# Short fp32 products of an attention and mixture-of-experts kernel issued as two halves of 64 stationary columns

## The chip, the cores and the metric

The kernel runs on one core of one Trainium2 chip, in one launch. The metric is the device time of that launch in microseconds (us); the median of three runs of the kernel before is 623.5 us (621.27 to 625.68).

## The reference

```python
def phi(x):                                   # x: (2, 8, 576, 64), scaled
    proj = np.einsum('bhsd,md->bhsm', x, omega)
    h = proj - np.sum(x * x, axis=-1, keepdims=True) / 2.0
    return np.exp(h - np.max(h, axis=-1, keepdims=True)) / np.sqrt(m)
kv = np.einsum('bhsm,bhsd->bhmd', k_p, v);  z = np.sum(k_p, axis=2)
num = np.einsum('bhsm,bhmd->bhsd', q_p, kv)
den = np.einsum('bhsm,bhm->bhs', q_p, z)[..., None] + 1e-06
x = (num / den)                               # laid out as 1152 tokens x 512
...
mask = e_idx == e                             # first expert layer: 8 experts, top 1
out[mask] = gate_w[mask, None] * eom[mask, e, None] * (np.maximum(x[mask] @ w1[e], 0.0) @ w2[e])
...
out += p[:, e:e + 1] * (np.maximum(x @ w1[e], 0.0) @ w2[e])   # second layer: 4 experts, all tokens
```

Everything is float32, with m = 128 features, 1152 tokens of 512 numbers and a hidden width of 1024.

## The kernel before

Most products are made from a high and a low part of each operand, as three fp32r products (`mm3`, lines 594 to 598; stage b, lines 295 to 297). A few are left as plain fp32 products, and these are what the change touches. A plain fp32 product shows in the trace as two passes, each with a weight load and a matmul.

The attention runs first. Its work goes in banks of 2 heads x 2 row sets for q and k, by batch b and half of the heads hh. `stage_a` transposes raw q or k (line 273) into the PSUM tile pt. `stage_b` multiplies with omega into pj (lines 295 to 297); VectorE takes the maximum and ScalarE the exponential (line 312). `kv_part` (line 326) sums k'v and z for four heads in the bank kv: the stationary operand is e, rows x 128 features, the moving one is v with a column of ones, 65 columns; the last 64 rows of a sequence (vr) go the same way with 64 rows. `kv_evac` copies the sum to kvs. `stage_cq` transposes the features of q (line 357), and `stage_d` (line 374) multiplies them with kvs into pnd, 65 columns again, divides, writes x to the DRAM tile xs and transposes it (line 385) into xh and xl. For the last 64 rows stage_d uses 64 stationary columns.

Then come the experts of the first layer, in chunks of 288 tokens: `l1` (tile ph), `l2_block` (tile py). One pair of a chunk and an expert with at most 64 tokens is gathered: line 805 picks the token rows with a one-hot matrix og into px (three token tiles x four column blocks), line 824 makes the first layer phx from raw fp32 weights xw1, line 832 the second, yx, and `scatter` (line 842) puts it back. Line 832 sends even f to output partitions 0 to 63 and odd f to 64 to 127:

```python
p0 = SLOTS * (f % 2)
mm = nc.tensor.matmul(yx[p0:p0 + SLOTS], hx[:, f], xw2[f // 4][:, f % 4, :], start=f < 2, stop=f >= FB - 2)
```

The buffers st of xw1 are reused for the second layer's weights xw2, whose DMAs (line 123) therefore wait for the products of line 824. A loop over the remaining pairs follows under a branch on nx (line 858), then the second expert layer (tiles pp and po).

The order of the instructions on each engine is made when the program is built, by a scheduler with its own costs, within the dependences; on the chip each engine takes them in that order.

Of the kernel before, what the change touches and what calls it, by code (L numbers as in the profile page):

```python
# [24 lines left out]
KB, FB = DM // 128, FF // 128  # L25
# [9 lines left out]
MXS = 8  # L35
SCALE = 1.0 / (D ** 0.25)
SLOT_J = (0, 2, 1, 3)


@with_exitstack  # L40
def moe_stack(ctx, tc, q, k, v, omega, w_gate, w_ogate, mw1, mw2, dprobs, dw1, dw2, out):
    nc = tc.nc
    TT, STT, TS = nc.vector.tensor_tensor, nc.vector.scalar_tensor_tensor, nc.vector.tensor_scalar

    def f32(ap):
        return ap.bitcast(F32)
# [97 lines left out]
    G = H // 2  # L144
# [135 lines left out]
    kvps = {}  # L280
# [41 lines left out]
    kvs = {}  # L322

    def kv_part(key, e, v65, first, last, r0, r1):
        for i in range(G):
            nc.tensor.matmul(kvps[key][:, i, :], e[i][r0:r1], v65[i],
                             start=first and i == 0, stop=last and i == G - 1)

    def kv_rest(b, hh):
        r = slice(64 * b, 64 * b + 64)  # L330
        vr = raw["v", 2]
        kv_part((b, hh), heads("k", 2, hh, 0), [vr[r, G * hh + i, :] for i in range(G)], False, True, r.start, r.stop)

    def stage_ck(u):
        kind, b, hh, j = u
        if b == 2:
            return kv_rest(0, hh)
        if j == 0:
            kvps[b, hh] = kbank[:, 0:G * (D + 1)].rearrange("p (g d) -> p g d", g=G)
        v65 = raw["v", b, hh]  # L340
        kv_part((b, hh), heads(*u), [v65[:, i, j, :] for i in range(G)], j == 0, False, 0, 128)
        if b == 1 and j == 3:
            kv_rest(1, hh)
# [21 lines left out]
    def stage_d(b, hh, u):  # L365

        t = st_e["T", u]
        rest = u[1] == 2
        m = 64 if rest else 128
        c0 = 64 * b if rest else 0  # L370
        bank = ps_n.tile([128, 512], F32, tag="nd", name="pnd")
        ps = bank[:, 0:G * (D + 1)].rearrange("p (g d) -> p g d", g=G)
        for i in range(G):
            nc.tensor.matmul(ps[:m, i, :], t[:, i, c0:c0 + m], kvs[b, hh][:, i, :], start=True, stop=True)

        rd = ap.tile([128, G], F32, tag="rd", name="rd", bufs=4)
        TS(rd[:m], ps[:m, :, D], M * 1e-6, None, op0=ALU.add)
        nc.vector.reciprocal(rd[:m], rd[:m])
        xn = ap.tile([128, G, D], F32, tag="xn", name="xn", bufs=4)
        TT(xn[:m], ps[:m, :, 0:D], rd[:m].unsqueeze(2).to_broadcast([m, G, D]), op=ALU.mult)  # L380
        dst = xs[8, 64 * b:64 * b + 64] if rest else xs[4 * b + SLOT_J[u[3]]]
        nc.sync.dma_start(dst[:, 256 * hh:256 * hh + 256], xn[:m].rearrange("p g d -> p (g d)"))
        px = bank[:, 0:256].rearrange("p (g n) -> p g n", g=2)
        for g in range(2):
            nc.tensor.transpose(px[:, g, :m], xn[:m, 2 * g:2 * g + 2, :].rearrange("p a d -> p (a d)"), ident[:m, :m])
        kbs = slice(2 * hh, 2 * hh + 2)
        if rest:
            cols = slice(S * b, S * b + S)
            dh, dl = (z[:, kbs, cols].rearrange("p k (c n) -> p k c n", c=2)[:, :, :, 256:NC] for z in (xh, xl))
            src = px[:, :, 0:64].rearrange("p k (c n) -> p k c n", c=2)  # L390
        else:
            s = SLOT_J[u[3]]
            col = S * b + NC * (s // 2) + 128 * (s % 2)
            dh, dl = (z[:, kbs, col:col + 128] for z in (xh, xl))
            src = px
        nc.scalar.copy(dh, src)
        x_done[b, hh, u[1:]] = TT(dl, src, f32(dh), op=ALU.subtract)
# [144 lines left out]
    def do_d(u):  # L542
        kind, b, hh, j = u
        if kind == "k":
            return
        if b < 2:
            cur["d"] = (b, hh)
        stage_d(*cur["d"], u)
        if b == 1 and j == 3:
            stage_d(1, hh, ("q", 2, hh, 0))  # L550
        if hh == 1 and (b == 2 or (b == 1 and j == 3)):
            gate(cur["d"][0])

    for st in range(n + LAGD + 2):
        if st < n:
            kind, b, hh, jp, hp = banks[st]
            if b < 2 and jp == 0 and hp == 0:
                squares(kind, b, hh, nc.vector if (kind, b, hh) == ("k", 0, 0) else nc.gpsimd)
                if kind == "k" and (b, hh) != (0, 0):
                    i = 2 * b + hh + 1  # L560
# [33 lines left out]
    def mm3(ps, st_hl, mv_hl, start, stop):  # L594
        (sh_, sl_), (mh, ml) = st_hl, mv_hl
        nc.tensor.matmul(ps, sh_, mh, start=start, stop=False)  # L596
        nc.tensor.matmul(ps, sh_, ml, start=False, stop=False)  # L597
        nc.tensor.matmul(ps, sl_, mh, start=False, stop=stop)  # L598
# [166 lines left out]
    xw1 = X.raw1()  # L765
    xt = [xg_.tile([128, DM], F32, tag="xt", name="xt", bufs=3) for _ in range(3)]
# [25 lines left out]
    og = xg_.tile([128, 3, SLOTS], F32, name="og")  # L792
# [9 lines left out]
    px = ps_n.tile([128, KB, SLOTS], F32, tag="nd", name="px")  # L802
    for kb in range(KB):
        for t in range(3):
            nc.tensor.matmul(px[:, kb], xt[t][:, 128 * kb:128 * kb + 128], og[:, t], start=t == 0, stop=t == 2)
    xg = xg_.tile([128, KB, SLOTS], F32, name="xg")
    nc.scalar.copy(xg, px)
    psx = ps_t.tile([128, 3, 128], F32, tag="pt", name="psx")
# [5 lines left out]
    e = nc.values_load(le_t[0:1, 0:1], engines=[SP], min_val=0, max_val=NE - 1)  # L814
# [4 lines left out]
    for q in range(2):  # L819
        pool, tag = RINGS[q]  # L820
        ps = pool.tile([128, 4, SLOTS], F32, tag=tag, name="phx")
        for i in range(4):
            for kb in range(KB):
                nc.tensor.matmul(ps[:, i], xw1[q][:, kb, 128 * i:128 * i + 128], xg[:, kb], start=kb == 0, stop=kb == KB - 1)
        nc.scalar.activation(hx[:, 4 * q:4 * q + 4], ps, AF.Relu)
    xw2 = X.raw2()

# [30 lines left out]
    with tc.If(nx > 0, preferred_fallthrough_block=True, label="more"):  # L858
        with tc.For_i(0, nx, 1) as it:
# [10 lines left out]
            t = lp.tile([128, 4, 2, NE], F32, tag="xt", name="xt")  # L870
# [12 lines left out]
    e = nc.values_load(ei[1][0:1, 0:1], engines=[SP], min_val=0, max_val=NE - 1)  # L883
# [148 lines left out]
    def layer2(e, j, g, h, w2):  # L1032
        for t in range(GROUPS[g][1] // 64):
# [3 lines left out]
            for i in range(2):  # L1037
                mm3(po, (h[i][0][:, ts_], h[i][1][:, ts_]), w2[i], i == 0, i == 1)
            b, jj = T // 4, SLOT_J[T % 4]
            pc = pb[:, 4 * b + jj if T < 8 else 8, e:e + 1]  # L1040
# [14 lines left out]
    for p in range(0, 4 * NE2, 2):  # L1055
        ej = [divmod(p + i, 4) for i in range(2)]
        ws = {}
        for i, g in ((0, 0), (1, 0), (0, 1), (1, 1)) if p == 0 else ((0, 0), (0, 1), (1, 0), (1, 1)):
            e, j = ej[i]
# [39 lines left out]
```

## Time and profile before

| | |
|---|---|
| median of 3 runs | 623.5 us (621.27 to 625.68) |
| the profiled execution | 623.27 us, of which the span from the first to the last instruction is 621.2 us |
| mean granted TensorE clock | 0.994 of 2.4 GHz |
| PE busy, PEld busy | 604.8 us (97%), 553.0 us (89%) |
| DVE, ACT, POOL busy | 407.8, 257.4, 259.8 us |

PE is TensorE's matmuls, PEld its weight loads. A matmul's busy time includes its way through the array, so successive matmuls overlap and the distance from start to start tells what one costs. In a name such as `kv<-v,e` the tile written stands first. `128*64 128x65` means 128 rows and 64 columns of stationary operand, and 65 moving columns on 128 partitions. Attention lies from the start to about 116 us, the first chunk of the first expert layer to about 150, the gathered pair from there to 184, the rest after that.

### The profile page before, as it was taken

The page shows a single profiled execution, that of the slowest core. Times are in us where ns is not written, and L with a number is a line of the kernel's source. Part 1 is how long each engine was busy: PE and PEld are TensorE (multiplying, and loading weights), DVE is VectorE, ACT ScalarE, POOL GpSimd, SP SyncE. Part 2 cuts the span into 40 slices and gives each one's busy share as a digit, 9 for nine tenths or more (in the row PEclk, how much of TensorE's full clock was granted, in tenths as well). Part 3 has the DMA queues.
Part 4 walks back from the last instruction along what each step waited for, and adds up shares of the span by engine and source line. Part 5 has one row for each costly group of instructions (what it writes and reads, how often), then busy time and mean ns, then how long its engine had stood idle before and what let it go on. Part 6 is the DMA issues. An engine that isn't in the chain of part 4 may idle for free.

```text
span 621.2 us, 10506 instructions
## 1 busy us (share of the span) xinstructions
PE 604.8 (97%) x3910; PEld 553.0 (89%) x3911; DVE 407.8 (66%) x937; ACT 257.4 (41%) x628; POOL 259.8 (42%) x302
## 2 busy tenths in 40 slices
PE   7989999999999998999999999999999999999996
PEld 6878899899969998999998998998998998998995
DVE  7686675886325588966676676676666666666564
ACT  4566676603214144544443443442442442442230
POOL 4995014400000004285753753753754754754220
PEclk9999999999999999999999999999999999999999
DMA  8731145007607020102202202102202202200004
GB/s 198 166 103 47 31 154 174 23 1 255 203 6 270 1 69 31 40 0 69 69 0 69 69 2 68 69 2 68 69 1 69 68 2 69 68 1 2 1 1 152
DMA packets 41238, 42.77 MB, mean 69 GB/s; under 512 B 14816, under 2 KB 29408, under 8 KB 41184
## 3 DMA queue, kind: packets, MB, share of 16 engines
q1 hardware_dynamic: 40896, 42.00, 21.5%
q8 instruction: 32, 0.52, 0.4%
q14 instruction: 22, 0.18, 0.1%
q10 hardware_dynamic: 288, 0.07, 0.0%
HBM read 37.34 MB, written 4.72 MB: 68 GB/s over the span
## 4 chain that ended last, share of the span: by engine, by line
PE 68%; DVE 1%; issue 0%; ACT 0%; ACTq 0%
PE po L597 11%; PE po L596 11%; PE po L598 11%; PE pp L596 9%; PE pp L598 9%; PE pp L597 9%; PE ph L596 1%; PE py L596 1%; PE py L598 1%; PE ph L598 1%; PE ph L597 1%; PE py L597 1%; DVE xcl L92 0%; DVE x2T L664 0%; DVE xl L92 0%; PE pg L629 0%
## 5 line engine op out<-in xcount | busy, mean ns | idle before, releaser
L92 POOL TENSOR_TENSOR wlo<-st,whi 128x512 fp32r<-128x512 f32 x100 | 120.6, 1229 | 228.6 <-ACT whi L91 223.8
L1044 DVE SCALAR_TENSOR_TENSOR oacc<-po,pb,oacc 128x512 f32<-128x512 f32 x135 | 99.9, 747 | 55.9 <-PE po L598 55.9
L91 ACT CAST whi<-st 128x512 fp32r<-128x512 f32 x120 | 67.9, 592 | 115.5 <-PE po L598 49.2
L597 PE MATMUL po<-wlo,hh 128*128 128x512 f32 x288 | 112.4, 390 | 0.0
L596 PE MATMUL po<-whi,hh 128*128 128x512 f32 x288 | 112.4, 390 | 0.0
L598 PE MATMUL po<-whi,hl 128*128 128x512 f32 x288 | 112.0, 389 | 0.0
L592 POOL TENSOR_TENSOR hl<-c,hh 128x320 fp32r<-128x320 f32 (+1 forms) x64 | 52.7, 824 | 87.0 <-ACT hh L591 74.0
L596 PE MATMUL pp<-xh,whi 128*128 128x320 f32 (+1 forms) x256 | 76.1, 297 | 0.0
L598 PE MATMUL pp<-xh,wlo 128*128 128x320 f32 (+1 forms) x256 | 76.1, 297 | 0.0
L597 PE MATMUL pp<-xl,whi 128*128 128x320 f32 (+1 forms) x256 | 76.1, 297 | 0.0
L598 PEld LDWEIGHTS po<-whi,hl 128*128 128x128 f32 x288 | 54.1, 188 | 11.3
L597 PEld LDWEIGHTS po<-wlo,hh 128*128 128x128 f32 x288 | 54.2, 188 | 10.1
L596 PEld LDWEIGHTS po<-whi,hh 128*128 128x128 f32 x288 | 54.2, 188 | 10.0
L991 DVE TENSOR_TENSOR c<-u,pp 128x320 f32<-128x320 f32 (+1 forms) x96 | 43.3, 453 | 22.1 <-PE pp L598 21.7
L596 PEld LDWEIGHTS pp<-xh,whi 128*128 128x128 f32 x256 | 48.8, 191 | 1.6 <-DVE u L1003 0.4
L597 PEld LDWEIGHTS pp<-xl,whi 128*128 128x128 f32 x256 | 48.8, 191 | 1.2
L590 ACT ACTIVATE c<-c 128x320 f32<-128x320 f32 (+1 forms) x64 | 28.5, 445 | 51.3 <-DVE c L991 50.5
L598 PEld LDWEIGHTS pp<-xh,wlo 128*128 128x128 f32 x256 | 48.8, 191 | 0.0
L312 ACT ACTIVATE e<-pj,nb 128x128 f32<-128x128 f32 x144 | 41.3, 378 | 15.7 <-DVE nb L305 14.8
L587 DVE SCALAR_TENSOR_TENSOR hl<-c,hh 128x320 fp32r<-128x320 f32 (+1 forms) x64 | 44.7, 733 | 0.2
L596 PE MATMUL ph<-xh,whi 128*128 128x288 f32 x128 | 38.2, 299 | 1.2 <-ACT dg L627 1.2
L596 PE MATMUL pp<-xch,whi 128*128 128x320 f32 (+1 forms) x128 | 38.1, 298 | 1.2 <-DVE c L991 1.2
(262 smaller groups left out, 1365.6 us busy)
## 6 DMA issues: line engine op xcount, KB each, us to landing
st<-in_moe_w_dram SPq DMA_DIRECT2D x32, 512.0 KB, 4.4
st<-in_moe_w_dram SPq DMA_DIRECT2D x10, 1024.0 KB, 5.6
v<-in_v_dram SPq DMA_DIRECT2D x16, 128.0 KB, 3.4
q<-in_q_dram SPq DMA_DIRECT2D x4, 512.0 KB, 4.7
xs<-xn SPq DMA_DIRECT2D x16, 128.0 KB, 1.7
own<-in_moe_w_dram SPq DMA_DIRECT2D x2, 1024.0 KB, 5.6
out_dram<-oacc SPq DMA_DIRECT2D x8, 256.0 KB, 2.1
k<-in_k_dram SPq DMA_DIRECT2D x3, 512.0 KB, 4.6
```

The lines of the kernel that those rows point to most:

```text
L91: nc.scalar.copy(hi, src)
L92: eng.tensor_tensor(lo, src, f32(hi), op=ALU.subtract)
L312: nc.scalar.activation(e[:, i // 2, i % 2], ps[:, i // 2, i % 2], AF.Exp, bias=nb[:, i // 2, i % 2:i % 2 + 1])
L587: STT(hl, src, 0.0, f32(hh), op0=ALU.max, op1=ALU.subtract)
L590: nc.scalar.activation(c, c, AF.Relu)
L592: nc.gpsimd.tensor_tensor(hl, c, f32(hh), op=ALU.subtract)
L596: nc.tensor.matmul(ps, sh_, mh, start=start, stop=False)
L597: nc.tensor.matmul(ps, sh_, ml, start=False, stop=False)
L598: nc.tensor.matmul(ps, sl_, mh, start=False, stop=stop)
L991: TT(c, u, p, op=op)
L1044: STT(oacc[:, T], po, pc, oacc[:, T], op0=ALU.mult, op1=ALU.add)
```

## The change

Four products with 128 stationary columns are each made as two with 64, the first for output partitions 0 to 63, the second for 64 to 127; the moving operand is the same for both. The products of line 374 for the last 64 rows had 64 columns already and stay.

```diff
+HALVES = (slice(0, 64), slice(64, 128))
...
     def kv_part(key, e, v65, first, last, r0, r1):
         for i in range(G):
-            nc.tensor.matmul(kvps[key][:, i, :], e[i][r0:r1], v65[i],
-                             start=first and i == 0, stop=last and i == G - 1)
+            for z in HALVES:
+                nc.tensor.matmul(kvps[key][z, i, :], e[i][r0:r1, z], v65[i],
+                                 start=first and i == 0, stop=last and i == G - 1)
...
         for i in range(G):
-            nc.tensor.matmul(ps[:m, i, :], t[:, i, c0:c0 + m], kvs[b, hh][:, i, :], start=True, stop=True)
+            for z in HALVES[:m // 64]:
+                nc.tensor.matmul(ps[z, i, :], t[:, i, c0 + z.start:c0 + z.stop], kvs[b, hh][:, i, :], start=True, stop=True)
...
         for t in range(3):
-            nc.tensor.matmul(px[:, kb], xt[t][:, 128 * kb:128 * kb + 128], og[:, t], start=t == 0, stop=t == 2)
+            for z in HALVES:
+                nc.tensor.matmul(px[z, kb], xt[t][:, 128 * kb + z.start:128 * kb + z.stop], og[:, t], start=t == 0, stop=t == 2)
...
             for kb in range(KB):
-                nc.tensor.matmul(ps[:, i], xw1[q][:, kb, 128 * i:128 * i + 128], xg[:, kb], start=kb == 0, stop=kb == KB - 1)
+                for z in HALVES:
+                    nc.tensor.matmul(ps[z, i], xw1[q][:, kb, 128 * i + z.start:128 * i + z.stop], xg[:, kb],
+                                     start=kb == 0, stop=kb == KB - 1)
```

On PE, the first k'v products (tile kv, from the features e of two banks) stand between the products with omega (tiles pj), before:

```order
L296 MATMUL pj_333<-oml_174,qTh_300 128x256
L326 MATMUL kv_181<-v0_120,e_201 128x65 x2
L326 MATMUL kv_181<-v0_120,e_226 128x65 x2
...
L297 MATMUL pj_333<-omh_173,qTl_301 128x256
L296 MATMUL pj_358<-oml_174,qTh_300 128x256
```

and after:

```order
L297 MATMUL pj_341<-oml_174,qTh_300 128x256
L328 MATMUL kv_181<-v0_120,e_201 64x65 x4
L328 MATMUL kv_181<-v0_120,e_226 64x65 x4
...
L298 MATMUL pj_341<-omh_173,qTl_301 128x256
L297 MATMUL pj_366<-oml_174,qTh_300 128x256
```

Eight products become sixteen in the same place, with the two halves of a product next to each other.

On PE, the first products of stage d (tiles pnd) lie among the transposes of q's features (tile pt, from e), before:

```order
L357 MATMUL pt_550<-ident_82,e_381 128x128 x2
L374 MATMUL pnd_564<-kvs_401,qpT_482 128x65 x4
L374 MATMUL pnd_579<-kvs_401,qpT_489 128x65 x2
L357 MATMUL pt_550<-ident_82,e_419 128x128
L374 MATMUL pnd_579<-kvs_401,qpT_489 128x65 x2
L295 MATMUL pj_535<-omh_173,qTh_453 128x256
```

and after:

```order
L359 MATMUL pt_570<-ident_82,e_397 128x128 x2
L377 MATMUL pnd_584<-kvs_421,qpT_502 64x65 x8
L377 MATMUL pnd_603<-kvs_421,qpT_509 64x65 x2
L359 MATMUL pt_570<-ident_82,e_439 128x128
L377 MATMUL pnd_603<-kvs_421,qpT_509 64x65 x5
L359 MATMUL pt_570<-ident_82,e_439 128x128
L377 MATMUL pnd_603<-kvs_421,qpT_509 64x65
```

Two stretches have become three (of 10, 5 and 1 halves), and one product's halves are parted.

On PE, the gathered pair's products px and phx stand among the second-layer products py, before:

```order
L805 MATMUL px<-og,xt 128x64
L596 MATMUL py<-hh,whi 128x288
L597 MATMUL py<-hl,whi 128x288
L805 MATMUL px<-og,xt 128x64
...
L805 MATMUL px<-og,xt 128x64 x10
L810 MATMUL psx<-ident,ogf 128x128
L598 MATMUL py<-hh,wlo 128x288
L596 MATMUL py<-hh,whi 128x288
L597 MATMUL py<-hl,whi 128x288
L824 MATMUL phx<-xg,st 128x64 x32
```

and after:

```order
L809 MATMUL px<-og,xt 64x64 x2
L599 MATMUL py<-hh,whi 128x288
L809 MATMUL px<-og,xt 64x64 x2
...
L809 MATMUL px<-og,xt 64x64 x20
L814 MATMUL psx<-ident,ogf 128x128
L601 MATMUL py<-hh,wlo 128x288
L599 MATMUL py<-hh,whi 128x288
L600 MATMUL py<-hl,whi 128x288
L829 MATMUL phx<-xg,st 64x64 x64
```

The places are nearly the same; px keeps three stretches and phx one.

## Rows read from the trace of the kernel before

**Rows 1.** The page: span, busy engines, and the chain by line.

```profile
span 621.2 us, 10506 instructions
...
PE 604.8 (97%) x3910; PEld 553.0 (89%) x3911; DVE 407.8 (66%) x937; ACT 257.4 (41%) x628; POOL 259.8 (42%) x302
...
PE po L597 11%; PE po L596 11%; PE po L598 11%; PE pp L596 9%; PE pp L598 9%; PE pp L597 9%; PE ph L596 1%; PE py L596 1%; PE py L598 1%; PE ph L598 1%; PE ph L597 1%; PE py L597 1%; DVE xcl L92 0%; DVE x2T L664 0%; DVE xl L92 0%; PE pg L629 0%
```

**Rows 2.** Busy us by stretch: length, PE, PEld, DVE, ACT, POOL (instructions), clock, DMA.

```profile
15.50:116.50 101.00, 96.49 (x771) 87.02 (x770) 70.24 (x242) 63.36 (x203) 48.63 (x67) 0.99 0.37 107
...
150.00:184.00 34.00, 33.86 (x240) 28.96 (x238) 12.20 (x39) 8.67 (x20) 0.00 (x0) 1.00 0.33 106
```

**Rows 3.** Waits of PE from 15.5 to 116.5 us: total, times, longest.

```profile
PE pj L295 <- ACT e L312: 1.9, 5, 0.6
PE pt L357 <- ACT e L312: 1.2, 3, 0.5
```

**Rows 4.** PE by shape, 15 to 116.5 us, then 150 to 185: busy us, mean ns.

```profile
L374 PE MATMUL pnd<-kvs,qpT 128*128 128x65 f32 x128 | 16.0, 271 | 0.0
L326 PE MATMUL kv<-v,e 128*128 128x65 f32 x128 | 15.6, 274 | 0.0
...
L326 PE MATMUL kv<-vr,e 64*128 64x65 f32 x32 | 4.4, 278 | 0.0
...
L824 PE MATMUL phx<-xg,st 128*128 128x64 f32 x64 | 7.4, 276 | 0.0
...
L805 PE MATMUL px<-og,xt 128*128 128x64 f32 x24 | 3.1, 271 | 0.0
```

**Rows 5.** Timeline of PE, 157.5 to 167 us: start, us, engine, line, tile, count.

```profile
158.74 7.36 PE L824 MATMUL phx<-xg,st 128*128 128x64 f32 x64
```

**Rows 6.** Timeline of PE around a stretch of k'v, 17.7 to 20.05 us.

```profile
17.84 0.28 PE L296 MATMUL pj<-oml,qTh 128*128 128x256 f32 x1
17.96 1.89 PE L326 MATMUL kv<-v,e 128*128 128x65 f32 x16
19.66 0.36 PE L297 MATMUL pj<-omh,qTl 128*128 128x256 f32 x1
```

**Rows 7.** Timeline of PE around stage d's last 64 rows, 44.05 to 45.3 us.

```profile
44.21 0.27 PE L273 MATMUL pt<-ident,qr 128*128 128x128 f32 x1
44.41 0.68 PE L374 MATMUL pnd<-kvs,qpT 128*64 128x65 f32 x8
45.02 0.33 PE L273 MATMUL pt<-ident,qr 128*128 128x128 f32 x1
45.19 0.38 PE L273 MATMUL pt<-ident,k 128*128 128x128 f32 x2
```

**Rows 8.** Timeline of PE around the first yx, 170.2 to 173.0 us.

```profile
170.34 0.30 PE L597 MATMUL py<-hl,whi 128*128 128x288 f32 x1
170.48 0.29 PE L598 MATMUL py<-hh,wlo 128*128 128x288 f32 x1
170.70 1.94 PE L832 MATMUL yx<-st,hx 128*64 128x512 f32 x8
172.57 0.40 PE L596 MATMUL py<-hh,whi 128*128 128x288 f32 x1
```

**Rows 9.** Timeline of PE, only what had started by 170.72 us.

```profile
170.70 0.65 PE L832 MATMUL yx<-st,hx 128*64 128x512 f32 x2
```

**Rows 10.** Timeline of PE, the products of scatter, 177.7 to 180.0 us.

```profile
177.92 2.10 PE L842 MATMUL pa<-back,ys 128*128 128x384 f32 x6
```

**Rows 11.** Timeline of SP's DMA issues, 155 to 185 us.

```profile
162.56 3.94 SPq L123 DMA_DIRECT2D st<-in_moe_w_dram  x2
```

**Rows 12.** DMA issues by tensor and size, the last number us from issue to landing.

```profile
st<-in_moe_w_dram SPq DMA_DIRECT2D x10, 1024.0 KB, 5.6
```

**Rows 13.** Timeline of PE, the second yx, 173.8 to 176.5 us.

```profile
174.23 1.94 PE L832 MATMUL yx<-st,hx 128*64 128x512 f32 x8
```

**Rows 14.** Timeline of PE after the branch, 183 to 186 us.

```profile
185.06 0.37 PE L596 MATMUL ph<-xh,whi 128*128 128x288 f32 x1 [1.21 <-ACT dg L627]
```

## The prediction

> **What bounds the kernel now.** I read the page first: its chain runs through PE's lines to the end, and PE is busy 97% of 621.2 us [rows 1]. A busy PE may still wait inside its matmuls, so I then read the stretches in which the changed products lie. From 15.5 to 116.5 us, the attention, PE is busy 96.5 of 101.0 us while DVE has 70.2 and ACT 63.4; from 150 to 184 us, the gathered pair, it is 33.9 of 34.0 [rows 2]. The waits of PE in the attention are five groups of 4.2 us together, the two largest 1.9 and 1.2, both for ScalarE's exponential [rows 3]. So PE sets the pace in both stretches, with other engines close behind in the first one. The reader is to see that a matmul less on PE counts here, but not all of it in the attention. The branch at 184 us is a fixed point: PE resumes at 185.06 us after it [rows 14], and all that follows is the same program, so what is gained or lost ahead of it is what the kernel gains or loses.
>
> **What a changed product costs now.** The shapes count the passes: 128 of pnd, 128 of kv with 128 rows, 32 of kv with 64 rows, 64 of phx, 24 of px, 376 in all [rows 4]. Their mean of 271 to 278 ns is no price, as they overlap. The distance is: 64 passes of phx in a row take 7.36 us, less the last one's 0.28, over 63, so 0.112 us each [rows 5]. The kv passes agree: sixteen from 17.96 until the next product really starts at 19.74 (19.66, plus 0.08 by which its 0.36 exceeds the usual 0.28) are 0.111 each, and neither end costs extra [rows 6]. That is 376 x 0.112 = 42.1 us of PE.
>
> What sets 0.112 is the weight load, not the 64 or 65 columns that stream: fp32 streams 384 columns in (2.10 - 0.49) / 5 = 0.322 us, 0.84 ns each, so 65 columns take 0.055 [rows 10]. With 64 stationary columns the load is shorter: stage d's last rows make 8 passes of 65 columns between 44.41 and 45.02; without 0.05 for the first load and 0.09 of the stretch's end (both below), 0.47 / 8 = 0.059 each [rows 7].
>
> **What two halves cost.** The trace has them: yx alternates the output halves. Two of its matmuls have started by 170.72, both from 170.70 [rows 9], and eight passes end after 1.94 us [rows 8]. One after the other, 512 columns at 0.84 ns would take 8 x 0.43 = 3.4 us; taking the last one's own 0.6 off, three more pairs take 1.34, 0.45 a pair. So two halves go through the array at once, with loads in parallel as well. But yx issues four instructions in 0.45 us, the new products would have to issue four in 0.06, and no row shows that pace. The bounds for a pair are therefore 0.055 us (the stream alone, both at once) and 2 x 0.059 = 0.118 (nothing overlaps, as in rows 7 where only one half exists). I take 0.060, near the row of one half, because the pairs of yx start at the same hundredth. A pair replaces a pass of 0.112: it saves 0.052, at the bounds from +0.057 to -0.006.
>
> **What each stretch adds.** Going between 128 and 64 stationary columns is not free. Before yx, the last py is streamed by 170.48 + 0.14 (the distance to its neighbour) = 170.62, and yx starts at 170.70: 0.08, then 0.05 for its first load (0.65 against 0.60). After it, the last pass begins at 172.05 and streams 0.43, and py comes at 172.57: 0.09, and 0.11 more for its load (0.40 against 0.29). Together 0.33 us [rows 8, 9]. Between transposes, which are 0.11 apart, it is 0.09 (44.32 to 44.41) + 0.05 + 0.09 + 0.06 (0.33 against 0.27) = 0.29 [rows 7]. Kv in its old shape paid nothing [rows 6]. In the new order, the changed products make 30 stretches in the attention (13 of kv, 17 of pnd, among them five of one half) and 4 in the gathered pair. Two of the kv stretches are the 64-row ones alone, which differ in shape from their neighbours before as well, and about three more border on a 16- or 64-row product that already changes the shape. So 25 new changes at 0.31 us are 7.8 us. Sixteen stretches or parts have an odd number, a half without partner: 16 x 0.058 = 0.9.
>
> **The sum on PE.** Attention: 288 x 0.052 = 15.0, less 7.8 and 0.9, is 6.3 us. Gathered pair: 88 x 0.052 = 4.6, less 4 x 0.33 = 1.3, is 3.3 us; almost all of it is the single long phx, px with stretches of 2, 2 and 20 halves comes out at zero.
>
> What is late next: in the attention, ACT's exponentials and DVE, which already hold PE 4.2 us and would be at 63 and 70 of 95 us instead of 101; DMAs of q, k and v land while PE works on the bank before. I count two thirds, 4.2 us; if the waits swallow all of it this is zero, with no wait it is 6.3. The order on the other engines changes in a few neighbours only, which I cost at nothing; at worst it adds a wait of the size of those in rows 3, 0.6 us. In the gathered pair no compute engine is near; but xw2's DMAs wait for phx. They are issued at 162.56 and 166.50 at the latest (3.94 for two) [rows 11] and a megabyte lands 5.6 us after its issue [rows 12], 172.1 against the second yx at 174.23 [rows 13], 2.1 us of slack. The second issue comes as much earlier as phx ends earlier, the first only half as much, so the two overlap more; both megabytes in sequence need about 10 us from the first issue, which leaves next to nothing. I take off 0.3, so 3.0 us. Behind yx nothing but PE's own queue waits.
>
> Sum: 4.2 + 3.0 = 7.2 us, less 0.4 for new waits of PE on fresh kvs and features when a stretch shrinks: 6.8. The profiled execution took 623.27 us (621.2 in the span and 2.1 around it), close to the median of 623.5, so the forecast is 623.3 - 6.8 = 616.5 us.
>
> **Rivals.** First, the halves don't overlap because PE can't issue faster. In rows 7 a load and a matmul come every 0.059 us, the fastest steady pace in the trace; if that is the pace of issue and not of the load, a pair costs 0.118. Then the attention gains 288 x -0.006 = -1.7, the gathered pair -0.5, and the changes of shape cost 7.8 and 1.3 more: -11.3 us on PE, of which about nine tenths reach the end, 633.5 us. It decides from a pair of 0.085 us on, where the sum on PE is zero (376 x 0.027 = 10.1 saved, 7.8 + 0.9 + 1.3 spent). For it: no row with four short instructions so close. Against: yx's pairs start at one time, though they had 0.4 us to be prepared. The Trainium skill has a rule of this kind ("TensorE: Matmul & The Clock Gate", section "Wait — 56ns, not 53.3ns?"): with hardware decode off, the sequencer spends about 62 ns on each matmul, which binds when the array needs less. By it a pair would take an estimated 124 ns and the kernel some 636 us; rows 7's pace lies just below 62, so the trace bears it out little, and its chance is inside the 0.2 of this rival.
>
> Second, the attention is held by ACT and DVE as soon as PE gets shorter, so only the gathered pair's 3.0 us come: 620.3 us. For it: the waits for exponentials exist already [rows 3]. Against: 4.2 us of waits in 101, and DVE has 30 us spare [rows 2]. A pair of some 0.08 us, between the bounds, lands there too: 376 x 0.032 = 12.0 saved, 10 spent, about 621.5.
>
> That the change doesn't do what it says is hardly a case: the order of the new program has the 64-column products.
>
> **Chances.** Forecast 0.55 (own range 612 to 620), gain lost in the attention or a pair in between 0.25, no overlap 0.2. A measurement of this kernel can tell about 1% (6.2 us) from no change. Of the forecast's 0.55, 0.42 lie below 617.3 and 0.13 in the band; of the second case 0.02 below, 0.20 in the band, 0.03 above; the third is above. That gives 0.44, 0.33, 0.23. The range reaches from 611.5 (all of the 9.6 us arrives and pairs take 0.055, 376 x 0.005 = 1.9 more) to 632, into the no-overlap case.
>
> **What would show it.** Right: phx as 128 passes in a stretch of about 4 us instead of 7.4, two matmuls of it starting within 0.01 us; gaps of 0.09 us at both ends of each kv and pnd stretch; the branch 6 to 7 us earlier. Wrong: phx in 7 to 8 us, that is passes 0.055 to 0.06 apart in single file, or changes of shape that cost other than 0.3; more PE waits for the exponential than 4.2 + 3 us would show the second rival; a wait of yx above 0.5 us would show the DMA term mis-sized.

## The result and the profile after

The changed kernel takes 613.64 us in the median of 4 runs (612.78 to 614.45), the kernel before 623.13 us beside it (621.27 to 625.68, 4 runs): a ratio of 0.9845 with a 95% interval of 0.9806 to 0.9883. That is 9.5 us or 1.55% faster, against a forecast of 6.8 us; the time lies inside the forecast's range of 611.5 to 632 us. The interval is a gain of 7.3 to 12.1 us, so 6.8 is a little too small.

The page of the changed kernel, its span and its busy engines:

```profile
span 612.6 us, 11258 instructions
...
PE 592.9 (97%) x4286; PEld 536.7 (88%) x4287; DVE 408.5 (67%) x937; ACT 257.3 (42%) x628; POOL 259.6 (42%) x302
```

There are 376 matmuls more than in [rows 1], PE is busy 11.9 us less, and the other engines work as long as before. The two stretches of [rows 2], the first now 6 us shorter, the second 6.5 us earlier and 2 us shorter (length, then busy us of PE, PEld, DVE, ACT, POOL, the clock and the DMA):

```profile
15.50:110.50 95.00, 89.35 (x1059) 75.55 (x1059) 70.91 (x242) 63.40 (x203) 49.27 (x67) 0.99 0.41 116
143.50:175.50 32.00, 30.81 (x331) 25.56 (x329) 12.44 (x39) 9.08 (x21) 0.00 (x0) 1.00 0.34 120
```

The waits of PE in the first of them, as in [rows 3], and the wait of yx in the second (engine, line waited for, total us, times, longest):

```profile
PE pj L296 <- ACT e L313: 3.0, 7, 0.9
PE pt L359 <- ACT e L313: 1.0, 2, 0.8
...
PE yx L838 <- DMA st<-in_moe_w_dram: 0.8, 2, 0.7
```

With 0.5, 0.4, 0.3, 0.2 and 0.2 in smaller groups, the waits of the attention are 5.6 us instead of 4.2: 1.4 more, where the forecast let others swallow 2.1. The wait of yx did not exist before.

PE by shape, as in [rows 4] (count, then busy us and mean ns of one), and the timeline of phx, as in [rows 5] (start, length, engine, line, tile, count):

```profile
L328 PE MATMUL kv<-v,e 128*64 128x65 f32 x256 | 9.9, 226 | 0.0
...
L377 PE MATMUL pnd<-kvs,qpT 128*64 128x65 f32 x288 | 14.4, 227 | 0.5 <-DVE xl L400 0.5
```

```profile
152.00 0.29 PE L600 MATMUL py<-hl,whi 128*128 128x288 f32 x1
152.23 3.95 PE L829 MATMUL phx<-xg,st 128*64 128x64 f32 x128
156.11 0.75 PE L632 MATMUL pg<-dg,ones 128*128 128x288 f32 x2
```

Phx has twice the passes in 3.95 us instead of 7.36. Less the last one's 0.22 and over 127 distances that is 0.029 us a pass, 0.059 a pair: the sum took 0.060, and the bounds were 0.055 and 0.118. The first stretch of k'v, to hold against [rows 6]:

```profile
17.90 0.37 PE L296 MATMUL pj<-omh,qTh 128*128 128x256 f32 x1
18.10 0.28 PE L297 MATMUL pj<-oml,qTh 128*128 128x256 f32 x1
18.32 1.15 PE L328 MATMUL kv<-v,e 128*64 128x65 f32 x32
19.40 0.39 PE L298 MATMUL pj<-omh,qTl 128*128 128x256 f32 x1
```

Before, it took 17.96 to 19.74, 1.78 us. Now it takes from 18.32 to 19.51 (19.40, and 0.11 by which 0.39 exceeds the usual 0.28), 1.19 us, and starts 0.22 after the neighbour's start instead of the 0.12 of [rows 6], 0.10 later. It saves 0.49 us; the sum gives 16 x 0.052 - 0.31 = 0.52. So both prices were right where they can be read directly. Split up, the 1.19 us are 16 pairs at 0.059, 0.94, and 0.25 for the first load, the stretch's end and the next load; with the 0.10 ahead a stretch pays 0.35 us.

### The profile page after: what moved, and what is told of

Its sections match the earlier page's. It is cut to its first block, busy times and chain, and to the rows that moved or that the text cites. A ratio compares the mean times of both kernels' runs of the same rounds, so it can differ in the third digit from the quotient of the medians.

```text
span 612.6 us, 11258 instructions
## 1 busy us (share of the span) xinstructions
PE 592.9 (97%) x4286; PEld 536.7 (88%) x4287; DVE 408.5 (67%) x937; ACT 257.3 (42%) x628; POOL 259.6 (42%) x302
## 4 chain that ended last, share of the span: by engine, by line
PE 67%; DVE 2%; DMA 1%; issue 0%; ACT 0%; SPq 0%
PE po L599 11%; PE po L601 11%; PE po L600 11%; PE pp L599 10%; PE pp L601 10%; PE pp L600 10%; PE py L599 1%; PE py L601 1%; DMA st<-in_moe_w_dram 1%; PE py L600 1%; PE ph L600 1%; PE ph L601 1%; PE ph L599 1%; DVE xcl L93 0%; DVE wlo L93 0%; DVE x2T L667 0%
```

## A table by fixed points

Four landmarks stand in each program: the 29th pass of `pj<-omh,qTh`, the first py, the first ph behind the branch, and the last po. Before and after, the first three of them are these rows of the timeline; the third row of before is [rows 14].

```profile
39.22 0.38 PE L295 MATMUL pj<-omh,qTh 128*128 128x256 f32 x1 [0.60 <-ACT e L312]
...
126.60 0.51 PE L596 MATMUL py<-hh,whi 128*128 128x288 f32 x1
```

```profile
38.42 0.38 PE L296 MATMUL pj<-omh,qTh 128*128 128x256 f32 x1 [0.28 <-ACT e L313]
...
120.50 0.51 PE L599 MATMUL py<-hh,whi 128*128 128x288 f32 x1
...
176.33 0.37 PE L599 MATMUL ph<-xh,whi 128*128 128x288 f32 x1 [1.20 <-ACT dg L630]
```

The stretches between the landmarks in the profiled execution of each kernel, in us (A: span's start to the 29th pass, B: from there to py, C: py to ph, D: ph to the last po):

```
                          A       B       C       D
before                  39.22   87.38   58.47   431.02
changed                 38.42   82.08   55.83   431.16
changed, again          36.09   82.13   54.89   431.19
k'v only                37.51   82.91   58.43   430.47
stage d only            37.24   86.74   58.45   431.10
gathered pair only      37.40   87.37   55.40   430.83
single file             38.15   86.63   56.07   431.30
k'v mixed               39.57   88.10   58.47   430.70
k'v and pair            36.13   82.85   54.79   430.71
yx later                38.80   82.08   54.45   430.85
yx later, again         38.10   82.06   54.45   430.77
k'v and pair, yx later  38.48   82.92   54.45   430.94
stage d grouped         37.22   83.23   56.05   431.09
```

Kernels that share the program of a stretch share its length in B to 0.1 us; in C too, where yx doesn't wait. D is the same for all to 0.9 us. A is not a fair measure: before and the gathered pair alone share its program, and are 1.8 us apart; the changed kernel, its second profile and the two with yx later share theirs, and are up to 2.7 us apart (36.09 to 38.80). For before and the gathered pair alone, the views by stretch show where it arises. Before, from 10 us on (length; PE, PEld, DVE, ACT, POOL; granted clock; DMA):

```profile
10.00:13.40 3.40, 1.17 (x8) 0.77 (x6) 3.08 (x13) 2.38 (x9) 1.71 (x7) 1.00 1.00 250
13.40:16.80 3.40, 3.08 (x15) 3.09 (x16) 1.79 (x6) 2.83 (x10) 2.92 (x2) 0.50 1.23 254
```

and the gathered pair alone:

```profile
10.00:13.40 3.40, 1.98 (x15) 1.53 (x13) 3.10 (x13) 2.26 (x9) 1.38 (x5) 1.00 1.09 238
13.40:16.80 3.40, 2.39 (x18) 2.06 (x18) 2.58 (x8) 3.32 (x11) 2.61 (x2) 1.00 1.21 248
```

In the one, PE was busy 1.17 us of 3.40 and then ran 3.4 us at a granted clock of 0.50, which is 1.2 GHz; in the other it was busy 1.98 us and stayed at 2.4 GHz. The busy time of that stretch alone doesn't tell the two cases apart, for the changed kernel's second profile has it busy 1.21 us and no fall either:

```profile
10.00:13.40 3.40, 1.21 (x8) 1.00 (x9) 2.98 (x11) 2.70 (x10) 1.46 (x6) 1.00 1.06 244
13.40:16.80 3.40, 2.87 (x28) 2.45 (x28) 2.83 (x8) 3.40 (x13) 3.24 (x3) 1.00 1.24 267
```

Its first profile had such a stretch:

```profile
14.70:18.10 3.40, 3.40 (x17) 3.22 (x16) 1.89 (x5) 2.56 (x8) 3.24 (x3) 0.50 1.16 224
```

Between before and the gathered pair alone, the slow stretch accounts for less than half of the 1.8 us. K'v begins at 17.96 us before [rows 6] and at 17.23 in the gathered pair alone, and stage d still at 29.26 and 28.53: 0.73 behind. The other 1.1 us come between there and 34 us, at full clock, where the kernel before waits for exponentials and the gathered pair alone has no wait of PE:

```profile
31.26 0.33 PE L357 MATMUL pt<-ident,e 128*128 128x128 f32 x1 [0.55 <-ACT e L312]
...
33.74 0.84 PE L357 MATMUL pt<-ident,e 128*128 128x128 f32 x3 [0.30 <-ACT e L312]
```

Whether these waits follow from the slow stretch isn't shown. The nearest there is to a fair comparison of A is between the executions without that stretch: 37.40 (gathered pair alone, its attention that of before) against 36.13 and 36.09, an estimated gain of 1.3 us from three executions. It is no more than that: stage d alone ran at 0.50 from 10.3 to 13.7 us and has 37.24.

The changed kernel's gain is then about 1.3 in A, 5.3 in B (87.38 to 82.08 and 82.13), and 2.6 to 3.6 in C (58.47 to 55.83 and 54.89): 9.2 to 10.2 us, around the 9.5 measured. B and C are sure to 0.1 us but for the wait of yx, A is not.

## The experiments

The theory was the forecast's: a pass of 0.112 us becomes a pair of 0.06, each stretch pays for two changes of the column count, and PE's pace decides. The rivals were the halves in single file, and an attention held by other engines.

**One part at a time.** Three kernels, each with halves in one part and the others as before. K'v only:

```diff
-            nc.tensor.matmul(kvps[key][:, i, :], e[i][r0:r1], v65[i],
...
+            for z in HALVES:
+                nc.tensor.matmul(kvps[key][z, i, :], e[i][r0:r1, z], v65[i],
...
```

> Only k'v is made as two halves (160 of the 376 passes). Theory (two halves run through the array at once, 0.058 us a pair, each change of shape costs about 0.3 us, and PE sets the end): 160 x 0.054 = 8.6 us saved, 13 stretches of which 8 or 9 bring a new change of shape at 0.33, 2.9, and 0.3 for odd halves: 5.4 us, so 617.7. Rival (the other engines hold the attention, two thirds arrive): 3.6 us, 619.5.

Measured: 616.46 us, ratio 0.9877 [0.9846, 0.9908], a gain of 5.7 to 9.6 us: above the 5.4 of the theory, and well above the rival's 3.6. B has 4.47 of it; how much of the rest is scatter of A isn't known. Stage d only:

```diff
-            nc.tensor.matmul(ps[:m, i, :], t[:, i, c0:c0 + m], kvs[b, hh][:, i, :], start=True, stop=True)
+            for z in HALVES[:m // 64]:
+                nc.tensor.matmul(ps[z, i, :], t[:, i, c0 + z.start:c0 + z.stop], kvs[b, hh][:, i, :], start=True, stop=True)
```

> Only stage d (num and den) is made as two halves (128 passes in 17 stretches). Theory: 128 x 0.054 = 6.9 us saved, 17 x 0.31 = 5.3 for changes of shape and 0.6 for halves without partner: 1.0 us, so 622, no difference that can be told. Rival (a change of shape costs nothing because PE waits there anyway): 6.3 us, 617.

Measured: 621.94 us, ratio 0.9973 [0.9941, 1.0005]. The gathered pair only (px and phx):

```diff
...
-                nc.tensor.matmul(ps[:, i], xw1[q][:, kb, 128 * i:128 * i + 128], xg[:, kb], start=kb == 0, stop=kb == KB - 1)
+                for z in HALVES:
+                    nc.tensor.matmul(ps[z, i], xw1[q][:, kb, 128 * i + z.start:128 * i + z.stop], xg[:, kb],
...
```

> Only px and phx are made as two halves; the attention is that of the kernel before. Theory: px comes out at 0.3, phx saves 64 x 0.054 - 0.3 = 3.1, and the wait of yx for its weights takes about 1 back: 2.5 us, 620.6; phx in 4.0 us instead of 7.4. Rival (the weights of yx land no earlier, so the wait takes the rest): within 0.5 us of before.

Measured: 619.84 us, ratio 0.9948 [0.9897, 1.0000]. In its profile yx waits 0.5 us for its weights.

The times alone put k'v ahead of the rest, and the table sorts them: in B, k'v alone gains 4.47 us and stage d alone 0.64, both together 5.30; in C, the gathered pair alone gains 3.07, and the others nothing. The rival that other engines take back what k'v saves falls with it, as k'v alone keeps 4.47 us. K'v pays since its passes come in long stretches: in B, counted on PE, it replaces 120 passes for 8 added changes of shape, stage d 104 for 24 (rows or columns of the stationary operand change).

**Stage d taken out again.** The changed kernel with stage d as it was:

```diff
-            for z in HALVES[:m // 64]:
-                nc.tensor.matmul(ps[z, i, :], t[:, i, c0 + z.start:c0 + z.stop], kvs[b, hh][:, i, :], start=True, stop=True)
+            nc.tensor.matmul(ps[:m, i, :], t[:, i, c0:c0 + m], kvs[b, hh][:, i, :], start=True, stop=True)
```

> The changed kernel with stage d whole again (k'v and the gathered pair in halves). By the sum on PE stage d saves 128 x 0.052 = 6.7 us and spends 17 changes and 5 odd halves, 5.6 us, so leaving it out costs about 1 us: 614.6 us. If halving only stage d is worth nothing or a loss, 613.6 us or less.

Measured: 613.50 us, ratio 0.9832 [0.9792, 0.9872], not to be told from the changed kernel. By the mark set beforehand (613.6 us or less) stage d's halves would be worth nothing; but this profile has no wait of yx and the changed kernel's has one (C 54.79 against 55.83). B is 82.85 instead of 82.08: stage d's halves are worth 0.8 us there, as little as the sum said (1 us), and too little for the times to show.

**The price of a change of shape.** Halves for two heads of four in each call of `kv_part`, from the kernel before, so that the shape changes inside every stretch:

```diff
+            if i < G // 2:
+                for z in HALVES:
+                    nc.tensor.matmul(kvps[key][z, i, :], e[i][r0:r1, z], v65[i],
...
+            else:
+                nc.tensor.matmul(kvps[key][:, i, :], e[i][r0:r1], v65[i],
```

> The kernel before, with halves in k'v for two of the four heads of each call, so that the change of shape falls inside every stretch of k'v. If a change of shape costs PE about 0.3 us wherever it stands: 80 passes are replaced at 0.052 each, 4.2 us saved, and some 20 changes spent, 6 us, so 1 to 2 us slower than before and about 8 us slower than k'v halved everywhere. If changes of shape hide in waits of PE, the 4.2 us arrive: about 619.5 us.

Measured: 624.68 us against 624.23 beside it, ratio 0.9999 [0.9973, 1.0025]. The 4.2 us of the passes are gone; a loss of 1 to 2 us is not resolved by the times, but in B there is one: 88.10 against 87.38, 0.72 us slower. The timeline of the first stretch:

```profile
18.15 0.28 PE L297 MATMUL pj<-oml,qTh 128*128 128x256 f32 x1
18.36 0.45 PE L329 MATMUL kv<-v,e 128*64 128x65 f32 x8
18.74 0.66 PE L332 MATMUL kv<-v,e 128*128 128x65 f32 x4
19.33 0.45 PE L329 MATMUL kv<-v,e 128*64 128x65 f32 x8
19.72 0.66 PE L332 MATMUL kv<-v,e 128*128 128x65 f32 x4
20.18 0.36 PE L298 MATMUL pj<-omh,qTl 128*128 128x256 f32 x1
```

Four pairs and four whole passes, twice, would need 8 x 0.058 + 8 x 0.112 = 1.36 us; from 18.36 to 20.26 they take 1.90 (20.18, and 0.08 more for the load). The 0.54 between go to three changes inside and to the first load of the one at the start (at the end, whole passes border on a product of 128 columns). With the 0.09 by which the first pass starts late (18.36, 0.21 behind its neighbour instead of 0.12) it is 0.63 for four changes, 0.16 each, the 0.155 of the forecast. Together with k'v only, two equations in B give what both prices are worth there: 120 p - 8 c = 4.47 and 60 p - 26 c = -0.72 give p = 0.046 us saved for a pass and c = 0.134 us for a change (two of them to a stretch: 0.27). For the changed kernel, 224 passes and 32 changes, they give 10.3 - 4.3 = 6.0, less 10 x 0.058 = 0.6 for the ten odd halves in B, 5.4; measured 5.3. The two prices, 0.046 and 0.134, are some seven eighths of those read directly, 0.052 and 0.155. The Trainium skill ("TensorEngine Tiling (Array Packing)", section "Key Properties") says that a change of the tiling mode drains TensorE, with no size. The traces agree in that each change costs time, 0.16 us read directly and 0.134 net here; that a drain is what it goes to, they don't show.

**Single file.** The changed kernel with the two loops exchanged, the first halves of a group before the second ones, in all four products:

```diff
...
-            for kb in range(KB):
-                for z in HALVES:
+            for z in HALVES:
+                for kb in range(KB):
...
```

> The same 64-column products as in the changed kernel, but all first halves of a group (4 heads, 3 token tiles, 4 column blocks) ahead of all second halves, so that neighbours in the queue use the same half of the array. Theory (the gain is that neighbours run at once): passes 0.058 apart in single file, a pair 0.117, 376 x -0.005 = -1.9 us, and the changes of shape cost 8 to 9 more: 633, slower than before by 10. Rival (the gain is that a load of 64 columns is short, whatever stands beside it): 614 as the changed kernel. Rival (the queue lets later halves pass earlier ones): also 614.

Measured: 618.70 us, ratio 0.9911 [0.9879, 0.9943]: neither the theory's 633 nor the rivals' 614, but in between. Phx in this kernel:

```profile
156.75 4.99 PE L829 MATMUL phx<-xg,st 128*64 128x64 f32 x128
```

Alternating halves took 3.95 us; in single file without any overlap 127 x 0.058 + 0.22 = 7.6 would be needed. Start times on PE show how it got to 4.99: where one half's group of eight passes ends, pairs of starts 4 to 6 ns apart appear, and eight passes come every 0.29 us instead of every 0.46. About (0.46 - 0.29) / 0.058 = 3 passes of the next half have begun beside the last three of the one before. Which half a start belongs to isn't in the trace; it is inferred from the spacing: with every start in the program's order, only the first of eight could stand beside a pass of the other half, and eight would take 7 x 0.058 = 0.41. So the order of issue matters, and alternating is worth 4.55 us in B (86.63 against 82.08).

**The wait of yx.** The changed kernel with the third block of the second layer ahead of yx:

```diff
-    next(blocks)
-    next(blocks)
+    for _ in range(3):
+        next(blocks)
     ys = second()
     next(blocks)
-    for d in range(3):
+    for d in range(KB):
         scatter(ys, d)
-    next(blocks)
-    scatter(ys, 3)
```

> The changed kernel with the third block of the second layer placed ahead of yx instead of behind it, so that yx's weights have landed when PE comes to it. If yx's wait for its DMA cost the changed kernel what the trace names (0.8 and 0.7 us of waits), the stretch from the last lgt to the last pa shrinks by 0.7 to 1.5 us from 62.6, and the time is about 612.6 us. If the wait was covered, or the block that was moved waits for something itself, the stretch stays at 62.6 and the time at 613.6.

Measured: 613.03 us, ratio 0.9812 [0.9776, 0.9849], and C is 54.45, 1.4 us below the changed kernel. Then both once more, on one chip:

> The changed kernel unaltered, beside the two others on one chip. If the wait of yx for its weights is a matter of how the DMAs fall in an execution, the stretch from the first py to the first product behind the branch takes anything from 54.8 us (no wait) to 56.1 us; if it belongs to the program, it takes 55.8 us again. The attention's stretch from the 29th product of omega with q's high part to the first py should be 82.1 us again, and the time 613.0 to 614.3 us.

> The changed kernel with the third block of the second layer ahead of yx, beside the changed kernel on one chip. The wait cannot arise, so the stretch from the first py to the first product behind the branch is 54.4 to 54.5 us again; the time is 0.4 to 1.4 us below the changed kernel of the same call, if what is won there is kept to the end.

Measured: the changed kernel 611.73 us (ratio 0.9810 [0.9773, 0.9847]), with yx later 612.29 us (0.9805 [0.9768, 0.9841]): no difference that can be measured, where yx later was expected to be 0.4 to 1.4 us ahead; and the changed kernel came out below the 613.0 to 614.3 expected of it. The timelines tell why. The changed kernel's first profile:

```profile
161.15 2.04 PE L838 MATMUL yx<-st,hx 128*64 128x512 f32 x8 [0.16 <-DMA st<-in_moe_w_dram]
...
165.22 1.94 PE L838 MATMUL yx<-st,hx 128*64 128x512 f32 x8 [0.66 <-DMA st<-in_moe_w_dram]
```

and its second:

```profile
158.66 2.04 PE L838 MATMUL yx<-st,hx 128*64 128x512 f32 x8
...
162.01 1.94 PE L838 MATMUL yx<-st,hx 128*64 128x512 f32 x8
```

The second yx starts 4.07 us behind the first in one execution and 3.35 in the other. The two issues of xw2, one a megabyte, on SP's queue of the first profile and of the second, are these:

```profile
154.35 2.24 SPq L124 DMA_DIRECT2D st<-in_moe_w_dram  x2
```

```profile
152.07 2.24 SPq L124 DMA_DIRECT2D st<-in_moe_w_dram  x2
```

The second megabyte lands at 165.09 and 161.83, 10.7 and 9.8 us after the first of these issues, 0.13 and 0.18 us ahead of the second yx. The same program waits or doesn't, by how its DMAs fall, and C goes from 54.8 (k'v and pair, no wait) to 55.8. Yx later takes the chance out and gains 0.4 on the luckiest case. That 0.4 is no wait, but about what one stretch less is worth (0.33), for the two groups of yx now follow each other:

```profile
164.49 3.65 PE L838 MATMUL yx<-st,hx 128*64 128x512 f32 x16
```

**Without stage d, yx later.**

```diff
-            for z in HALVES[:m // 64]:
-                nc.tensor.matmul(ps[z, i, :], t[:, i, c0 + z.start:c0 + z.stop], kvs[b, hh][:, i, :], start=True, stop=True)
+            nc.tensor.matmul(ps[:m, i, :], t[:, i, c0:c0 + m], kvs[b, hh][:, i, :], start=True, stop=True)
...
-    for d in range(3):
+    for d in range(KB):
...
```

> K'v and the gathered pair in halves, stage d whole, and the third block of the second layer ahead of yx. From the traces so far: stage d's halves are worth 0.8 us between the 29th product of omega with q's high part and the first py, so this should end 0.8 us behind the changed kernel with yx later in that stretch, 82.9 against 82.1 us, and gain as much as that one from the first py to the first product behind the branch, 54.4 us. If both are true, the time is 612.9 to 613.9 us. If the 0.8 us is jitter, the stretch is 82.1 us.

Measured: 613.19 us, ratio 0.9822 [0.9786, 0.9858]; B is 82.92 and C 54.45, both as foretold.

**Stage d in fewer stretches.** The changed kernel with stage d's products held behind the last transpose:

```diff
...
-            nc.tensor.transpose(ps[:, i, :], e[i], ident)
+            last_t[0] = nc.tensor.transpose(ps[:, i, :], e[i], ident)
...
+        with tc.issue_after(last_t[0].ins):
...
```

> The changed kernel with stage d's products kept behind the last transpose of the features they use, so that they make 14 stretches instead of 17 and no half stands alone but for the last rows. Three changes less at 0.3 us and five odd halves less at 0.06 us: about 1.2 us faster, 612.4 us, if PE alone sets the pace of the attention; the products come later, so if the DVE work behind them (division, transposes of x) is what is waited for then, no gain or up to 1 us slower, 613.6 to 614.6 us.

Measured: 613.13 us, ratio 0.9813 [0.9777, 0.9849]: no measurable gain. Its B is 83.23, with five transposes of q more than the changed kernel's, an estimated 5 x 0.11 = 0.55 us by the distance in [rows 7]. Without them it is some 0.6 us longer, though four changes and six odd halves fewer should have saved 0.9. So grouping didn't pay here; why not stays open.

No version tried beats the changed kernel by more than a measurement can tell. By the traces, yx later is the best, by 0.4 to 1.4 us in C.

## Why the prediction was right, and where its size was off

- **A pair costs 0.060.** Right: 0.059 in phx. The first rival, a pace of issue of 0.059 us for a load and a matmul, falls: two loads and two matmuls come every 0.059 us. The Trainium skill's rule ("TensorE: Matmul & The Clock Gate", section "Wait — 56ns, not 53.3ns?"), 62 ns for each matmul with hardware decode off, doesn't bind here: 128 matmuls came 29 ns apart in the mean.
- **A stretch pays 0.29 to 0.33.** Right to 0.05: 0.35 in the stretch shown, 0.16 for a change with k'v mixed, 0.27 a stretch net from two experiments.
- **The sum on PE, 6.3 us in the attention.** 5.3 in B, which is sure, and some 1.3 in A, which is an estimate: 6.6 together.
- **"I count two thirds, 4.2 us."** This term is the one that was mis-sized. In B alone, the prices of the forecast give 224 x 0.052 - 32 x 0.155 = 6.7, less 0.6 for odd halves, 6.1, and 5.3 came: seven eighths. The waits there grew by 0.8 us, from 2.7 to 3.5, which is the difference. ACT and DVE were close, but 4.2 us of waits in 101 was the better guide (and the argument I gave against the second rival). That rival falls with the kernel of k'v alone, which gains 4.47 us in B.
- **Px at zero.** Small miss: from the first px to the first phx it is 4.61 us before and 4.16 after, 0.45 gained.
- **"I take off 0.3" for yx.** Right in mechanism ("next to nothing" of slack, both megabytes about 10 us from the first issue: 9.8 and 10.7), uncertain in size: C gains 3.6 us where yx doesn't wait and 2.6 in the first profile, against 3.0 forecast.
- **0.4 for new waits.** They belong to the 0.8 above.
- **Nothing behind the branch.** Right: D is 431.02 before and 431.16 after.
- **The range from 611.5 us.** By its own terms (9.6 and 1.9) it should begin at 611.8; nothing hangs on it.

Taken together: 9.6 us on PE were worked out and 6.8 forecast; 9.5 came, and 11.9 when the changed kernel was measured again (623.61 to 611.73). The discounts for what might be late next were the error, not the prices. That the 9.6 and the 9.5 agree so closely is in part luck: the profile behind the 9.5 has a wait of yx that others lack, and A scatters.

## What to carry to other kernels

A short fp32 product with 128 stationary columns and some 64 moving ones is bound by its stationary side here: a pass takes 0.112 us, one of 64 stationary columns 0.059, and the moving columns alone 0.055. Two halves of 64 columns, issued alternately, run side by side at about half the cost, 0.059 a pair. Each stretch of them pays about 0.3 us where its neighbours have 128 columns, which a saving of 0.05 us a pass earns back from about six passes on, so halve what comes in long stretches; grouping short ones was tried once and gained nothing. And where the bounding engine is busy nearly throughout and waits a few per cent, don't take off a third of the gain worked out on it without a row that says so: here some seven eighths arrived.

## What the runs showed that was not expected

- Two matmuls and two loads issued in 0.059 us, and passes of the next column half beginning about three ahead, beside the last ones of the half before, when the halves aren't alternated.
- A stretch of 3.4 us (in one case 6.8) at a granted clock of 0.50 before the 29th pass in ten of the thirteen profiled executions and not in three; PE's busy time from 10 to 13.4 us does not tell them apart. Executions of one program differ by up to 2.7 us before the 29th pass. In the pair that was compared, 0.73 of 1.8 us lie around this stretch and 1.1 in a later one at full clock, with waits for exponentials; what starts either isn't known.
- The landing of two megabytes behind each other varied by about 1 us between executions of one program, enough to make a wait or none.
